# One dense tile of short pieces instead of two, with the tests' classification and the fetched rows' copies moved

## The chip, the cores and the metric

The kernel runs on one core of a Trainium2 chip. The metric is the device time of one execution in microseconds; three executions are quoted by their median. One further execution was profiled, and every row below is from that one.

## What is computed

Attention over 4 sequences of 768 tokens and 8 heads of 64 (a causal window of 128 keys, and 4 sink keys that every query sees), then a soft mixture of experts, then a mixture in which each token goes to one expert:

```python
x = attention(q, k, v)                      # 3072 x 512
logits = x @ phi                            # 8 experts x 4 slots
slot_in = softmax(logits, axis=0).T @ x     # 32 x 512
slot_out[e] = relu(slot_in[e] @ w1[e]) @ w2[e]
x = softmax(logits, axis=1) @ slot_out      # 3072 x 512

idx = argmax(normed(x) @ normed(expert_emb).T / tau)
p = softmax of those logits at idx
out = p * (relu(x @ w1[idx]) @ w2[idx])     # float32
```

After the soft mixture every row of x is a combination of the same 32 slot rows, and with the reference's inputs all 3072 tokens choose the same expert in the second mixture.

## The kernel before

The first 200 us are the attention and the soft mixture; the change touches them in one place, `tokens()`, which puts the combining weights of the tokens into the order of the output tiles. The rest is the second mixture for the one chosen expert, and its method sets the words used below.

The combining weights stand in `cstack` (96 rows that carry a high and a low part, 32 rows that are filled late), a column for each of the 3072 tokens, in 24 tiles of 128. The expert's first layer, pulled through the slots, stands in `gst`. So a product of a 128-column piece of `gst` with 512 columns of `cstack` gives the hidden layer before its relu for 128 units and 512 tokens. That is a **test** (`hidden()`, T, L1192): 8 unit groups f by 6 token groups g, 48 in all. The kernel doesn't keep the hidden layer. It counts signs: `sign(n)` (c0 to c47) goes over the test on ScalarE (Sign with an accumulated sum, L1201) or VectorE (L1203), by the list `ON_ACT`. A unit that is positive for every token counted is linear, and needs no relu; one that is positive for none is left out; the others are **mixed**.

Early tokens see few keys, and their hidden layer has many sign changes. The first `ND` = 2 tiles are therefore **dense**: tile 0 and tile 1 hold the first 64 tokens of each of the four sequences, and their signs are not counted. Their relu is kept by `relu_d()` (h, L1209, ScalarE) and its rounding rest by `rest_d()` (i, L1216, VectorE), in two parts of `hd`; `products()` (D, L1228) multiplies them with the expert's whole second layer, 24 products for a tile. Tiles 2 and 3 hold the second 64 tokens of each sequence, tiles 4 to 23 are 128 rows in a row each. `rows_of(t)` tells which rows of the output a tile stands for: two pieces of 64 rows for tiles 0 to 3, else one of 128.

**Classification** is made in two parts, `ca` for the first `NA` = 5 unit groups and `cb` for the other three: a reduction of the counts and comparisons on VectorE (L1249 to L1253), a product on POOL, two on TensorE that number the mixed units, and `pos` on VectorE (L1262). `select(f)` (e0 to e7) turns a group's numbers into a matrix of 0 and 1; `gather()` (L1279) multiplies those with `gt`, so that up to 256 columns hold the mixed units' first layer, copied to `gc` by ScalarE (L1281). `SEL_ACT` = (7,) puts the last select onto ScalarE, as two operations. `rows()` (L1288) brings the numbers into a column, `fetch()` makes indices of them (`ii`, L1304, VectorE) and issues two indirect DMAs on POOL (L1307), which read the mixed units' rows of the second layer into `w2g`: first 128, and in the second half at most 10 more. `split_rows()` copies and splits them (w2c, ScalarE L1311 and VectorE L1313; `wx`, ScalarE L1315, and part of `gws`, VectorE L1317). `linear()` (lin) sums the linear units on TensorE (8 products, L1326), copies on ScalarE (L1328, L1334) and finishes `gws` on VectorE (L1336).

Output tiles 2 to 23 are made by `outputs(t)` (y2 to y23): four products into one PSUM bank (L1382), three with `w2c` and the mixed units' hidden layer of this token group (`hm`, made by `mixed(g)`: TensorE L1348, ScalarE L1350, VectorE L1352), and a fourth with `gws` and `cstack`, whose last 32 rows `extra(g)` writes (TensorE L1361, ScalarE `hx` L1364, VectorE L1366). The last tile is made in two halves of 256 columns (L1378). `stores()` (st) takes the tiles in order: ScalarE evicts with the gate as its scale into one of six buffers `ot` (L1234), and SyncE issues one DMA for each piece of `rows_of(t)` (L1236).

Every engine works in order. PSUM is eight banks handed out first in, first out by `take()` and `give()`. The order is written by hand: each name in the string `ORDER` advances that generator to its next `yield`, so a step that stands early in the string stands early on its engine. At the end, when the count of mixed units is over `CAP` = 138, or when tokens have other experts, a branch ("rest") does the remaining work.

## Time and profile before

| | us |
|---|---|
| three executions | 277.50, 277.81, 278.89; median 277.81 |
| the profiled execution | 277.48 |
| its span | 275.7 |
| TensorE busy in the span | 260.6 (95%) |
| ScalarE, VectorE, POOL busy | 193.6, 184.4, 168.7 |
| the tests | 211 to 234 |
| first product with gws | 249.19 |
| last product | 268.54 |

The whole span's shares are a mean over stages with different limits: attention, the soft mixture, the tests, the chain from the last classification to `gws`, and the output. What a step is worth has to be read in its stage, by what waits and for whom. The durations of a row are of the one profiled execution.

### The profile page before, as it was taken

To read this page: it belongs to the slowest core of one execution; us is meant where nothing else is said; L and a number is where in the kernel's file an instruction comes from. 1 tells how busy PE (TensorE), PEld (TensorE's weight loads), DVE (VectorE), ACT (ScalarE), POOL (GpSimd) and SP (SyncE) were. 2 spreads that over 40 slices of the span, in tenths; PEclk is the share of its full clock that TensorE was granted. 3 is DMA by queue.
4 is the path that set the end of the run, shared out by engine and by line. 5 is a ranking of instruction groups with operands and counts; after the bars stand their busy time and mean duration, and the time that the engine had idled before them with its cause. 6 is when DMAs were issued, how large, how long until landed. Compare 5 with 4: busy or idle time off the path is not lost. (4 is left out here: it accounts for less than half of the span.)

```text
span 275.7 us, 8854 instructions
## 1 busy us (share of the span) xinstructions
PE 260.6 (95%) x3257; PEld 165.7 (60%) x3257; DVE 184.4 (67%) x556; ACT 193.6 (70%) x679; POOL 168.7 (61%) x394
## 2 busy tenths in 40 slices
PE   7987989999999999999999999999999999999990
PEld 5645646665666665666655563333477774777880
DVE  6786768888888898887985144526326889673410
ACT  2676988889898898989988522311227998677981
POOL 4398999999999999999999440001203995110000
PEclk9999999999999999999999999999999999999997
DMA  7894598756797467889924498999059000036884
GB/s 242 307 421 172 182 349 295 253 153 217 295 410 253 146 194 231 313 283 370 411 81 152 134 424 316 420 440 393 13 185 407 19 1 1 2 94 146 306 293 160
DMA packets 15198, 65.37 MB, mean 237 GB/s; under 512 B 2736, under 2 KB 3248, under 8 KB 11568
## 3 DMA queue, kind: packets, MB, share of 16 engines
q1 hardware_dynamic: 13600, 63.77, 62.7%
q10 hardware_dynamic: 1392, 0.48, 0.7%
q8 instruction: 27, 0.44, 0.6%
q0 software_dynamic: 160, 0.52, 0.6%
q14 instruction: 19, 0.16, 0.2%
HBM read 58.48 MB, written 6.29 MB: 235 GB/s over the span
## 5 line engine op out<-in xcount | busy, mean ns | idle before, releaser
L255 ACT ACTIVATE pr<-sc,nm 128x132 f32<-128x132 f32 x192 | 68.6, 373 | 5.8 <-DVE rs L260 3.8
L265 POOL TENSOR_TENSOR pr<-pr,rs 128x528 f32<-128x528 f32 x48 | 51.2, 1067 | 10.4 <-DVE rs L261 9.7
L233 DVE COPY_PREDICATED sc<-t_le_q,sc 128x512 f32<-128x512 uint32 x48 | 33.3, 695 | 10.1 <-PE sc L218 8.0
L255 ACT ACTIVATION_READ_ACCUMULATOR pr<-sc,nm 128x1 f32 x192 | 40.0, 209 | 0.0
L218 PE MATMUL sc<-qk 64*32 64x164 f32 (+4 forms) x1536 | 36.2, 294 | 2.1 <-DMA qk<-in_qkv_dram 1.9
L241 DVE TENSOR_REDUCE sc<-sc 128x4 f32<-128x528 f32 x48 | 33.9, 706 | 1.1
L289 ACT ACTIVATE raw<-m 128x512 f32<-128x512 f32 x48 | 28.6, 603 | 6.1 <-PE m L284 2.8
L295 POOL TENSOR_SCALAR_AFFINE_SELECT pt<-raw 128x512 f32<-128x512 f32 x48 | 30.6, 639 | 0.4
L339 PE MATMUL xa<-pt,v 128*64 128x256 f32 (+1 forms) x256 | 29.5, 361 | 0.7 <-POOL pt L299 0.7
L218 PEld LDWEIGHTS sc<-qk 64*32 64x32 f32 x1536 | 21.4, 106 | 14.4 <-issue 7.0
L284 PE MATMUL m<-ident,pr 128*128 128x128 f32 x192 | 28.9, 276 | 0.6 <-POOL pr L265 0.6
L284 PEld LDWEIGHTS m<-ident,pr 128*128 128x128 f32 x192 | 22.0, 141 | 4.1 <-POOL pr L265 2.1
L339 PEld LDWEIGHTS xa<-pt,v 128*64 128x64 f32 x256 | 15.6, 136 | 10.8 <-issue 3.3
L810 POOL CAST scr<-scr 128x256 fp32r<-128x256 f32 x6 | 2.4, 402 | 30.7 <-DVE scr L806 30.0
L373 ACT ACTIVATE xtok<-m 128x512 f32<-128x512 f32 (+1 forms) x32 | 15.8, 497 | 6.6 <-PE m L356 6.1
L302 POOL TENSOR_SCALAR_AFFINE_SELECT pt<-raw 128x256 f32<-128x256 f32 x48 | 19.5, 408 | 0.7
L339 PE MATMUL xb<-pt,v 128*64 128x128 f32 (+1 forms) x192 | 18.1, 315 | 0.0
L1169 POOL TENSOR_TENSOR w2h<-w2t,ones 128x512 fp32r<-128x512 f32 x8 | 8.3, 1042 | 15.3 <-PE b L1019 15.3
L356 PE MATMUL m<-ident,xt 128*128 128x128 f32 x96 | 15.8, 275 | 0.0
L1201 ACT ACTIVATE junk<-b 128x512 f32<-128x512 f32 (+1 forms) x26 | 14.8, 568 | 0.5
L1382 PE MATMUL b<-w2c,hm 128*128 128x512 f32 x45 | 14.7, 399 | 0.0
L339 PEld LDWEIGHTS xb<-pt,v 128*64 128x64 f32 x192 | 10.7, 136 | 5.0 <-issue 3.8
(327 smaller groups left out, 566.5 us busy)
## 6 DMA issues: line engine op xcount, KB each, us to landing
w<-in_m1w_dram SPq DMA_DIRECT2D x19, 1024.0 KB, 8.1
qk<-in_qkv_dram SPq DMA_DIRECT2D x15, 780.0 KB, 5.7
w<-in_m1w_dram SPq DMA_DIRECT2D x4, 2048.0 KB, 12.8
v<-in_qkv_dram SPq DMA_DIRECT2D x16, 448.0 KB, 3.5
out_dram<-ot SPq DMA_DIRECT2D x19, 256.0 KB, 2.6
x<-in_m1w_dram SPq DMA_DIRECT2D x4, 1024.0 KB, 8.1
w1t<-in_m2w_dram SPq DMA_DIRECT2D x4, 512.0 KB, 5.2
w2t<-in_m2w_dram SPq DMA_DIRECT2D x4, 512.0 KB, 8.9
```

Source lines behind the costliest of these rows:

```text
L218: pe.matmul(sc[r0:r0 + 32, h, o + lo:o + hi], lhsT=lhsT, rhs=qk[hp:hp + 64, k0 + lo:k0 + hi], start=True, stop=True)
L233: dve.copy_predicated(mv[:, :, :, 0:128], mk.to_broadcast([128, 2, 2, 128]), bv[:, :, :, 124:252])
L241: dve.tensor_reduce(mx, mv[:, :, :, 0:UW], axis=X, op=ALU.max, negate=True)
L255: act.activation(out=pr[:, h, i2, :], in_=mv[:, h, i2, 0:UW], func=AF.Exp, bias=nm[:, h, i2:i2 + 1], scale=0.125, accum_out=sm[:, h, i2, 0:1])
L265: pool.tensor_tensor(out=pr, in0=pr, in1=sm.rearrange("p h (i o) -> p h i o", o=1).to_broadcast([128, 2, 2, UW]), op=ALU.mult)
L284: pe.transpose(ps[:, h, i2, :], pr[:, h, i2, 0:128], ident)
L289: act.activation(out=raw, in_=tp_t.pop(u), func=AF.Copy)
L295: pool.affine_select(out=pt[:, :, :, 0, :], in_=raw_t[u], pattern=[[0, 2], [0, 2], [1, 128]], compare_op=ALU.is_ge, fill=0.0, base=0, chan ...
L302: pool.affine_select(out=pt_t[u][:, :, 0, 1, :], in_=raw_t[u][:, :, 1, :], pattern=[[0, 2], [-1, 128]], compare_op=ALU.is_gt, fill=0.0, ba ...
L339: pe.matmul(o[64 * h:64 * h + 64, c0:c0 + 128 * (l1 - l0)], lhsT=v[:, j, h, :], rhs=mv[:, h, 128 * l0:128 * l1], start=False, stop=last, s ...
L356: pe.transpose(ps[:, 128 * t:128 * t + 128], xt[:, 128 * (t0 + t):128 * (t0 + t) + 128], ident)
L373: act.activation(out=dst, in_=src, func=AF.Copy)
```

## The change

The dense tiles go from two to one. `rows_of` now lays tiles 0 to 3 out in four pieces of 32 rows: tile t holds tokens 32t to 32t+31 of each of the four sequences, so the dense tile 0 has the first 32 tokens of each, and tiles 1 to 3, now ordinary output tiles, the next 96. `tokens()` follows that layout. The relu and rest of the dense part go from 256 columns to 128, the first group's signs from 256 to 384, the dense products from 48 to 24 and the output tiles' products from 88 to 92. The output DMAs go from 29 to 36: 16 pieces of 32 rows and 20 tiles, where 8 pieces of 64 rows, 19 tiles and two halves stood; the last tile is made and stored whole. `NA` goes from 5 to 6, so that the first classification waits for six groups' signs and the second has two; the last select goes from ScalarE to VectorE. `ORDER` is written anew from the middle on. Lines 1192 to 1236 move by one or two and the outputs' line from L1382 to L1376.

```diff
-ND = 2
+ND = 1
+NF = 4

     def rows_of(t):
-        if t < 2 * ND:
-            h, b2 = divmod(t, ND)
-            return [(slice(64 * k, 64 * k + 64), S * (2 * b2 + k) + 64 * h, 64) for k in range(2)]
-        b, i = divmod(t - 2 * ND, NB - 1)
+        if t < NF:
+            return [(slice(32 * b, 32 * b + 32), S * b + 32 * t, 32) for b in range(B)]
+        b, i = divmod(t - NF, NB - 1)
         return [(slice(0, 128), S * b + 128 * (i + 1), 128)]

         def tokens(b2):
...
             for b in range(2):
-                for k in range(2):
-                    pe.matmul(tp[64 * b:64 * b + 64, 32 * k:32 * k + 32], lhsT=lt_all[:, 2 * b2 + b, 64 * k:64 * k + 64], ...)
+                r = 64 * b2 + 32 * b
+                for k in range(NF):
+                    pe.matmul(tp[r:r + 32, 32 * k:32 * k + 32], lhsT=lt_all[:, 2 * b2 + b, 32 * k:32 * k + 32], ...)
...
-            act.activation(out=c_tok[:, b2:b2 + ND + 1:ND, :], in_=tp[:, 0:64]..., func=AF.Copy)
+            act.activation(out=c_tok[rs, 0:NF, :], in_=tp[rs, 0:32 * NF]..., func=AF.Copy)
...
     def products():
-        for t in range(ND):
-            tok = slice(128 * t, 128 * t + 128)
-            y = hold(("y", t), 1)
-            for f in range(8):
-                for k, w in ((0, w2h), (0, w2l), (1, w2h)):
-                    pe.matmul(y, lhsT=hd[:, k, f, tok], rhs=w[:, f], ...)
+        ys = [hold(("y", t), 1) for t in range(ND)]
+        for f in range(8):
+            for k, w in ((0, w2h), (0, w2l), (1, w2h)):
+                for t in range(ND):
+                    pe.matmul(ys[t], lhsT=hd[:, k, f, 128 * t:128 * t + 128], rhs=w[:, f], ...)

-    def store(t, c):
+    def store(t):
-        act.activation(out=ot[:, c], in_=y[:, c], func=AF.Copy, scale=gsel[:, t:t + 1])
+        act.activation(out=ot, in_=y, func=AF.Copy, scale=gsel[:, t:t + 1])
         for ps, r, n in rows_of(t):
-            sp.dma_start(out=out[r:r + n, c], in_=ot[ps, c])
+            sp.dma_start(out=out[r:r + n, :], in_=ot[ps])

     def outputs(t):
-        if t == NTILE - 1:
-            for c in (slice(0, 256), slice(256, 512)):
...
-    SEL_ACT = (7,)
-    NA = 5
+    SEL_ACT = ()
+    NA = 6
     ORDER = """
...
-        c32 c33 c34 ca c35 h u0 ca w2 T T T D D c37 c38 ca ca i c36 c39 T D T T c40 T D T c41 c44 h e1 e0 T T c43 e2 D gat gat T gat e3 gat lin c45 c46 i c42
+        c35 ca h u0 ca w2 T T D T ca ca e0 e1 e2 c37 c38 i c36 c39 T D T T D c40 T T D c41 c44 h T T c43 gat gat T gat e3 gat lin c45 c46 c42 c47 cb e4 e5 D
...
```

The first place is TensorE around the end of the gather (L1279) and the rows (L1288); L1326 and L1332 are the linear part, L1361 and L1348 `extra` and `mixed`, `m` or a `b` with a number is a PSUM bank. Before:

```order
L1228 MATMUL m<-w2h,hd 128x512
L1279 MATMUL b_3980<-sel,gt 128x256 x3
L1326 MATMUL b_3988<-w2t,gta 32x512 x4
L1228 MATMUL m<-w2h,hd 128x512
L1228 MATMUL m<-w2l,hd 128x512
L1288 MATMUL b_4039<-ident,gc 128x1 x2
L1361 MATMUL b_4047<-cstack,gc 128x512
L1348 MATMUL b_4050<-cstack,gc 128x512
L1361 MATMUL b_4052<-cstack,gc 128x512
```

After, on the same engine:

```order
L1229 MATMUL b_3849<-w2l,hd 128x512
L1279 MATMUL b_3975<-sel,gt 128x256 x2
L1229 MATMUL b_3849<-w2h,hd 128x512 x2
L1288 MATMUL m<-ident,gc 128x1 x2
L1326 MATMUL b_3983<-w2t,gta 32x512 x4
L1348 MATMUL b_4040<-cstack,gc 128x512
L1361 MATMUL b_4042<-cstack,gc 128x512
L1229 MATMUL b_3849<-w2l,hd 128x512
L1332 MATMUL b_4045<-gwb,rep_153 128x512
```

The rows stand behind the gather and two dense products now, and the second half of the linear part, which stood ahead of them, behind; a single first `mixed` and `extra` go ahead of the linear part's last product.

The second place is ScalarE from the first fetched rows on (L1311, then L1315 `wx`), with L1334 a copy to `gws`, L1364 `hx`, L1350 `hm` and L1234 (after: L1235) the evictions of output tiles. Before:

```order
L1311 ACTIVATE w2c<-w2g 128x512
L1334 ACTIVATE gws<-b_4084 96x512
L1364 ACTIVATE hx<-b_4088,xm 32x512
L1234 ACTIVATE ot<-m,gsel 128x512
L1315 ACTIVATE wx_3633<-w2g,xm 32x512
L1234 ACTIVATE ot<-m,gsel 128x512
L1234 ACTIVATE ot<-b_4098,gsel 128x512
L1350 ACTIVATE hm<-b_4143 128x512
```

After, on the same engine:

```order
L1311 ACTIVATE w2c<-w2g 128x512
L1315 ACTIVATE wx_3641<-w2g,xm 32x512
L1334 ACTIVATE gws<-b_4045 96x512
L1364 ACTIVATE hx<-m,xm 32x512
L1350 ACTIVATE hm<-b_4087 128x512
L1235 ACTIVATE ot<-b_3849,gsel 128x512
L1235 ACTIVATE ot<-m,gsel 128x512
L1235 ACTIVATE ot<-b_4077,gsel 128x512
L1235 ACTIVATE ot<-b_4080,gsel 128x512
L1364 ACTIVATE hx<-b_4115,xm 32x512
```

`wx` stands directly behind the first fetched rows' copy, where `gws`, an `hx` and an eviction stood between; the dense tile's eviction, the first one, is behind all five.

The third place is SyncE's queue from the last weights to the branch at the end (`aint` is the branch's word). Before:

```order
L993 DMA w2t<-in_m2w_dram 128x1024
L1236 DMA out_dram<-ot 64x512 x8
L1236 DMA out_dram<-ot 128x512 x19
L1236 DMA out_dram<-ot 128x256 x2
L1577 TENSOR_LOAD aint
L1577 ISA x2
```

After, on the same engine:

```order
L995 DMA w2t<-in_m2w_dram 128x1024
L1237 DMA out_dram<-ot 32x512 x16
L1237 DMA out_dram<-ot 128x512 x20
L1571 TENSOR_LOAD aint
L1571 ISA x2
```

Eight pieces of 64 rows have become sixteen of 32, and the halves of the last tile are gone.

## Rows read from the trace of the kernel before

**Rows 1.** The page's first line.

```profile
span 275.7 us, 8854 instructions
```

**Rows 2.** Busy time by stretches: from:to, length, then each engine with its instructions.

```profile
core 0: us, PE busy (x) PEld busy (x) DVE busy (x) ACT busy (x) POOL busy (x), PEclk, DMA share, GB/s
163.00:190.00 27.00, 26.91 (x250) 10.19 (x248) 12.32 (x31) 5.99 (x13) 0.80 (x2) 1.00 0.97 397
222.20:233.80 11.60, 10.97 (x51) 7.34 (x51) 10.64 (x35) 11.19 (x36) 8.91 (x10) 1.00 0.00 1
249.20:268.90 19.70, 19.61 (x89) 15.95 (x89) 5.98 (x22) 16.67 (x27) 0.00 (x0) 1.00 0.78 256
```

**Rows 3.** Timeline, 236 to 250 us: start, duration, engine, line, operation, [idle before, releaser].

```profile
236.70 0.51 ACT L1270 ACTIVATE sel<-sq,ones 128x256 fp32r<-128x256 f32 x1
...
237.26 0.19 PEld L1279 LDWEIGHTS b<-sel,gt 128*128 128x128 f32 x1 [0.24 <-ACT sel L1270]
...
237.58 1.06 PE L1326 MATMUL b<-w2t,gta 128*32 128x512 f32 x8
...
239.68 0.34 DVE L1304 TENSOR_SCALAR ii<-b,ebase 128x1 int32<-128x1 f32 x2 [1.36 <-PE b L1288]
...
240.19 1.18 POOL L1307 DMA_INDIRECT w2g<-in_m2w_dram,ii  x1 [4.74 <-DVE cnt L1295]
...
241.68 0.95 POOL L1307 DMA_INDIRECT w2g<-in_m2w_dram,ii  x1 [0.30 <-issue]
...
243.72 0.63 ACT L1311 ACTIVATE w2c<-w2g 128x512 fp32r<-128x512 f32 x1 [0.61 <-DMA w2g<-in_m2w_dram,ii]
...
246.28 0.72 ACT L1315 ACTIVATE wx<-w2g,xm 32x512 fp32r<-32x512 f32 x1
...
248.44 0.69 DVE L1336 TENSOR_TENSOR gws<-b,gws 32x512 fp32r<-32x512 f32 x1
...
249.19 0.50 PE L1382 MATMUL b<-gws,cstack 128*128 128x512 f32 x1
...
249.73 0.69 ACT L1234 ACTIVATE ot<-b,gsel 128x512 f32<-128x512 f32 x1 [0.63 <-PE b L1382]
```

**Rows 4.** Timeline, 256 to 269 us, ScalarE and TensorE.

```profile
256.97 0.68 ACT L1364 ACTIVATE hx<-b,xm 32x512 fp32r<-32x512 f32 x1
...
268.54 0.27 PE L1378 MATMUL b<-gws,cstack 128*128 128x256 f32 x1
```

**Rows 5.** Tile `ot`, 263.4 to 270 us: ns min/median/max, first and last start; the landing.

```profile
L1236 SPq DMA_DIRECT2D out_dram<-ot x9: 332/383/1888, 263.6 to 269.8; - x9
...
DMA to landing us min/median/max: 2.9/3.9/4.3
```

**Rows 6.** Busy time by stretches of 1 us, columns as in rows 2.

```profile
251.00:252.00 1.00, 1.00 (x6) 0.82 (x5) 0.25 (x1) 0.88 (x2) 0.00 (x0) 1.00 0.97 203
258.00:259.00 1.00, 1.00 (x6) 0.82 (x5) 0.97 (x2) 0.97 (x3) 0.00 (x0) 1.00 0.97 363
265.00:266.00 1.00, 1.00 (x6) 0.82 (x5) 0.23 (x2) 0.87 (x2) 0.00 (x0) 1.00 0.11 33
```

**Rows 7.** Tile `ot`, 255.1 to 263.3 us, whole tiles of 128 rows.

```profile
L1236 SPq DMA_DIRECT2D out_dram<-ot x10: 332/332/333, 255.2 to 263.0; - x10
...
DMA to landing us min/median/max: 2.0/2.2/4.3
```

**Rows 8.** Tile `ot`, 249 to 253.4 us, pieces of 64 rows.

```profile
L1236 SPq DMA_DIRECT2D out_dram<-ot x6: 466/526/590, 249.1 to 252.8; - x6
...
DMA to landing us min/median/max: 2.2/2.3/2.4
```

**Rows 9.** Groups by line and form on ScalarE, 211.2 to 234.3 us: busy, mean ns.

```profile
L1201 ACT ACTIVATE junk<-b 128x512 f32<-128x512 f32 x22 | 13.2, 601 | 0.4
...
L1209 ACT ACTIVATE hd<-b 128x256 fp32r<-128x256 f32 x7 | 2.6, 378 | 0.0
L1201 ACT ACTIVATE junk<-b 128x256 f32<-128x256 f32 x4 | 1.5, 384 | 0.0
```

**Rows 10.** Tile `w2g`: the two indirect DMAs' landing.

```profile
DMA to landing us min/median/max: 3.5/3.6/3.8
```

More of the change, by code (lines that the diff above doesn't have):

```diff
@@ L751, in tokens @@
             tp = take()
+            rs = slice(64 * b2, 64 * b2 + 64)
+            for b in range(2):
+                r = 64 * b2 + 32 * b
+                for k in range(NF):
+                    pe.matmul(tp[r:r + 32, 32 * k:32 * k + 32], lhsT=lt_all[:, 2 * b2 + b, 32 * k:32 * k + 32], rhs=ident[0:96, 0:32], start=True, stop=True)
             for b in range(2):
                 for k in range(2):
-                    pe.matmul(tp[64 * b:64 * b + 64, 32 * k:32 * k + 32], lhsT=lt_all[:, 2 * b2 + b, 64 * k:64 * k + 64], rhs=ident[0:96, 0:32], start=True, stop=True)
-            for b in range(2):
-                for k in range(2):
-                    o = 64 + 192 * b + 96 * k
+                    o = 128 + 192 * b + 96 * k
                     pe.transpose(tp[:, o:o + 96], lt_all[:, 2 * b2 + b, 128 * k:128 * k + 128], ident[0:96, 0:96])
             yield
-            act.activation(out=c_tok[:, b2:b2 + ND + 1:ND, :], in_=tp[:, 0:64].rearrange("p (k s) -> p k s", k=2), func=AF.Copy)
+            act.activation(out=c_tok[rs, 0:NF, :], in_=tp[rs, 0:32 * NF].rearrange("p (k s) -> p k s", k=NF), func=AF.Copy)
             for b in range(2):
-                o = 64 + 192 * b
-                c0 = 2 * ND + 5 * (2 * b2 + b)
+                o = 128 + 192 * b
+                c0 = NF + 5 * (2 * b2 + b)
                 act.activation(out=c_tok[:, c0 + 1:c0 + 4:2, :], in_=tp[:, o + 32:o + 96].rearrange("p (g s) -> p g s", g=2), func=AF.Copy)
@@ L1222, in products @@
         hd, w2h, w2l = room("hd"), room("w2h"), room("w2l")
[L1223 to L1228 removed]
+        ys = [hold(("y", t), 1) for t in range(ND)]
+        for f in range(8):
+            for k, w in ((0, w2h), (0, w2l), (1, w2h)):
+                for t in range(ND):
+                    pe.matmul(ys[t], lhsT=hd[:, k, f, 128 * t:128 * t + 128], rhs=w[:, f], start=(f == 0 and k == 0 and w is w2h), stop=(f == 7 and k == 1))
                     yield
[L1231 removed]
+    def store(t):
         y = held["y", t]
         ot = Q.sb.tile([128, DM], F32, tag="ot", bufs=6, name="ot")
[L1234 removed]
+        act.activation(out=ot, in_=y, func=AF.Copy, scale=gsel[:, t:t + 1])
         for ps, r, n in rows_of(t):
[L1236 removed]
+            sp.dma_start(out=out[r:r + n, :], in_=ot[ps])
         drop(("y", t))
@@ L1240, in stores @@
         for t in range(NTILE):
-            for c in (slice(0, DM),) if t < NTILE - 1 else (slice(0, 256), slice(256, 512)):
-                store(t, c)
-                yield
+            store(t)
+            yield
     def classify(fs):
@@ L1372, in outputs @@
         tok = slice(128 * r, 128 * r + 128)
-        y = hold(("y", t), 1 if t < NTILE - 1 else 2)
+        y = hold(("y", t), 1)
         hm = hm_t[g]
-        if t == NTILE - 1:
-            for c in (slice(0, 256), slice(256, 512)):
-                for k, (a, b) in enumerate(((hm[:, 0, tok], Q.w2c[:, 0, c]), (hm[:, 1, tok], Q.w2c[:, 0, c]), (hm[:, 0, tok], Q.w2c[:, 1, c]), (cs_t[0][:, 128 * t:128 * t + 128], Q.gws[:, c]))):
-                    pe.matmul(y[:, c], lhsT=a, rhs=b, start=(k == 0), stop=(k == 3))
-                yield
-            return
         for k, (a, b) in enumerate(((hm[:, 0, tok], Q.w2c[:, 0]), (hm[:, 1, tok], Q.w2c[:, 0]), (hm[:, 0, tok], Q.w2c[:, 1]), (cs_t[0][:, 128 * t:128 * t + 128], Q.gws))):
@@ L1417, in kernel_body @@
-        c47 e4 cb cb D D D gat cb cb e7 e5 D D num D e6 gate gate gate gat gat gat lin D D gat gate row fetch fetch fetch fetch fetch x1 m1 x0 lin num gate x1
-        x1 x0 m1 m0 x0 m2 m2 m2 m0 m0 w2c D D D D D D lin lin D x2 D D D D x2 x2 w2c y2 y5 D D D y2 D y3 y5 y3 D D D y7 y2 D st w2c m1 w2c y3 y6 y4 lin y2 y5
-        y5 y6 st st m3 y4 y4 y3 y9 m3 m3 y7 y7 y10 y4 y6 y6 st st st x3 y8 y9 y8 x3 flag x3 y8 y8 y7 st st y15 x4 y10 y9 y9 y15 y12 y12 y13 m4 y13 st st x4
-        flag x4 m4 m4 y10 y10 y11 y13 y11 y11 y11 st st y16 y12 x5 y12 y15 y18 y13 y16 y14 y14 y14 y14 x5 st st st y16 y16 y15 m5 st flag x5 y18 y18 st m5 y17
@@ new lines, in kernel_body @@
+        cb D cb gat gat cb e6 e7 D num D gat gat i gate gate gat D D row fetch fetch fetch fetch fetch lin gate num gate lin m0 x0 D lin D m0 m0 x0 gate x0 m1
+        D D m1 m1 w2c D x1 w2c w2c lin lin w2c x1 x1 y1 y1 y2 y2 y3 y3 y4 y4 m2 y1 y2 m2 y3 y4 st m2 y1 st y2 st x2 y3 st x2 x2 y4 st y5 y5 y5 y5 st y6 y6 y6
+        y6 st y7 y7 y7 y7 st y8 y8 y8 y8 st y9 y9 m3 y9 y9 m3 m3 st y10 y10 x3 y10 y10 x3 x3 st flag y11 y11 y11 y11 st y12 y12 y12 y12 st y13 y13 m4 y13 y13
+        m4 m4 st flag y14 y14 x4 y14 y14 x4 x4 st y15 y15 y15 y15 st y16 y16 y16 y16 st flag y17 y17 m5 y17 y17 m5 m5 st y18 y18 x5 y18 y18 x5 x5 st flag y19
@@ L1422, in kernel_body @@
+        y19 y19 y19 st y20 y20 y20 y20 st flag hint y21 y21 y21 y21 st y22 y22 y22 y22 st y23 y23 y23 y23 st
         """.split()
```

10 lines of the change are left out of this document (4 added, 6 removed).

## Prediction, made before the changed kernel was run

> **What bounds the kernel now.** The profiled execution took 277.48 us, 0.33 below the median of the three runs (277.81); its span is 275.7 us [rows 1], so 1.78 lie outside the span. I sum against 277.48 and add the difference to the median at the end. About 0.5% (1.39 us) is what a measurement of this kernel can tell from no change.
>
> I read the busy time by stretches first. TensorE is busy 26.91 of 27.0 us while the soft mixture runs, 10.97 of 11.6 us in the tests, and 19.61 of 19.7 us in the output stretch [rows 2]. Its granted clock is 1.00, the higher of the two levels (2.4 GHz), in all three. In the tests stretch ScalarE (11.19 us) and VectorE (10.64 us) are as full as TensorE, so the eviction of the tests sets its pace. The reader should then see what starts the output stretch: a chain of small steps, pos, select, gather, gc, rows, ii, indirect fetch, w2c and gws, of which the last, VectorE's L1336, releases TensorE at 249.19 after 0.55 us of idling [rows 3]. From there TensorE streams to its last product at 268.54 [rows 4]; ScalarE evicts, SyncE issues the last store at 269.8 and the span ends 5.9 us later [rows 1, 5].
>
> One more engine hides in that stretch. The DMA engines are 0.78 busy on average [rows 2], and their speed depends on the piece. In 251 to 252 us, with 64-row pieces in flight, they are 0.97 busy for 203 GB/s; in 258 to 259, with whole tiles, 0.97 busy for 363 GB/s [rows 6]. A 64-row piece (131 kB) thus occupies them for 131/203 = 0.646 us, a 128-row tile (262 kB) for 0.72: half the rows cost nearly the whole time. SyncE's issue of one piece shows the same slope: 0.332 us for a whole tile [rows 7], 0.526 median and 0.590 at most for a 64-row piece [rows 8]. Before, eight such pieces pass without holding anybody up. After, there are sixteen of 32 rows.
>
> **The change part by part.**
>
> *The tests.* Relu of the dense part goes from 256 to 128 columns. From 601 ns at 512 columns and 384 at 256 [rows 9], a column costs 0.85 ns, 128 of them 0.108 us. Eight relus save 0.87 us on ScalarE, the four first-group signs there grow by 0.43, and VectorE's rest shrinks alike; 24 dense products of some 0.23 us leave TensorE, which has cover here. Against it, the first classification now sums six units' tests, two tests further, and its pos and three selects stand straight behind it on VectorE, ahead of tests c37 and c38, whose banks TensorE and ScalarE wait for. I take -0.2 us for the start of the second classification, with bounds of -0.8 (relu saving, half of it as VectorE's) and +0.3 (VectorE's idling for pos).
>
> *The last select.* Before, it is two ScalarE operations, the second 0.51 us from 236.70, and the gather's last weight load waits 0.24 us for it [rows 3]. On VectorE it is one operation behind the other selects, and TensorE works on dense products till then. I take -0.3: the wait and a hand-over.
>
> *The rows.* Before, their small products stand behind eight products of the linear part (1.06 us from 237.58) and dense products; VectorE's ii starts at 239.68 after 1.36 us of waiting for them [rows 3]. After, they stand behind the gather and two dense products (which cover the copy gc), and the second four linear products behind them. That gives -0.9 (those 1.06 less a hand-over); with the two terms above, -1.4, and the first indirect DMA at 240.19 - 1.4 = 238.8. The linear part loses 0.3 by it, but its result is wanted only at gws, later than the fetched rows.
>
> *Fetched rows ahead of other copies.* The first half of w2g is used 3.53 us after its issue (243.72 against 240.19), the second issue comes 1.49 after the first [rows 3], and the longer landing of the two is 3.8 [rows 10]: 238.8 + 1.5 + 3.8 = 244.1. Before, the copy wx waited until 246.28 behind an eviction and hx. After, wx follows at once (0.72), then the copy to gws (0.60), then VectorE's two subtractions of 0.69: 244.1 + 0.72 + 0.60 + 1.38 = 246.8, where 249.13 stood. So gws is ready 2.3 us earlier; 1.5 to 3 in bounds.
>
> *The tile more.* From the first gws product on, before has 82 products' worth in 268.54 - 249.19 + 0.12 = 19.5 us, 0.237 each [rows 3, 4]; after it has 86.5: 20.5 us. If nothing else waits, the stream ends at 246.85 + 20.5 = 267.35, 1.3 us earlier. The last tile is no longer in halves; its eviction starts 0.54 after its last product starts and takes 0.69 [rows 3]: 267.1 + 1.23 = 268.35. The last store then needs a landing. The last nine stores before took 3.9 us (median), behind one issue of 1.888 us [rows 5], during which the DMA engines stood nearly idle (0.11 in 265 to 266 [rows 6]); without that, 2.2 to 2.4 are usual [rows 7, 8]. With 2.4, then 2.0 from landing to the span's end (5.9 less 3.9) and 1.78: 274.5. That is the bound by TensorE alone.
>
> *The sixteen pieces.* ScalarE's queue after the second fetch is wx, gws, hx, hm and the dense tile's eviction; five at 0.60 back to back (the mean of 128x512 in rows 9) end at 247.15, when the first piece can be issued. Sixteen pieces at c each, the last landing 2.2 after its turn [rows 8], give 247.15 + 15c + 2.2 = 249.35 + 15c for the end of the four split tiles. There are six output buffers: tile 9 needs the buffer of tile 3. Behind tile 9's eviction on ScalarE stands hx of the fourth group (0.68 alone [rows 4], 0.60 back to back), behind that VectorE's 0.69 for cstack (the duration of L1336 [rows 3]), and behind that, on TensorE, the last product of tile 13 and all that follows. From that product's start to the last one's start are 42.5 products, 10.07 us. So the run is 249.35 + 15c, plus 2.0 (eviction, hx, cstack, hand-overs), plus 10.07 + 1.23 + 4.4 + 1.78, or 268.8 + 15c. It comes level with before at c = 0.58, is 0.5% faster below 0.485, 0.5% slower above 0.67, and TensorE's own bound takes over below 0.38.
>
> No row shows a 32-row piece. The bounds of c: below, a whole tile's issue, 0.332 [rows 7], and a gap that I estimate at 0.05, together 0.38; above, the step from 0.332 to 0.526 made once more, 0.72, with the gap 0.77. Between stand 0.57 (the 64-row issue [rows 8] with the gap) and 0.646 (the DMA engines' time for a 64-row piece, if a quarter of the rows again halves the speed). I take 0.62, next to the later of these two, since the queue is empty at the first pieces.
>
> The row above says that a half-height piece keeps the engines nearly as long as a whole tile. The Trainium skill has the same direction as a rule, in "DMA: Bandwidth & Descriptors", section "Rules for kernel authors": two transfers to disjoint halves of the partitions serialize, and one of 128 partitions should be used. It speaks against this change; it gives no price for a quarter.
>
> *At nothing.* tokens() makes 16 small products of 32 rows where 8 stood, and more evictions, while the weights' DMA is 0.97 busy [rows 2]; TensorE's other work there covers it too, and with both gone eight more small products cost some tenths. Waits of POOL and SyncE's queue elsewhere are not moved.
>
> **Sum.** 268.8 + 15 x 0.62 = 278.1, or 0.6 above 277.48; on the median's scale 278.4. Its own range, for c of 0.57 to 0.68 and the tests' bounds, is 276.9 to 279.5.
>
> **The rivals.**
>
> *Pieces overlap.* Four pieces of a tile touch four disjoint quarters, so they might run side by side, and an issue might cost what a whole tile's does. Then TensorE is the bound: 274.5, on the median's scale 274.8. For it: 0.332 is what nearly all whole tiles take [rows 7]. Against it: the 64-row pieces of one tile didn't overlap, 203 GB/s at 0.97 [rows 6]. The Trainium skill's linear law ("DMA: Bandwidth & Descriptors", section "Anatomy of one DMA", fitted for POOL's queue: some 2 us and bytes by 436 GB/s) would give 64 KB only 0.15 us of transfer, an estimate from that page, and so this case; the 203 GB/s of rows 6 already break it for pieces of 128 KB.
>
> *Pieces cost more still.* Fewer rows each time made the issue longer. At 0.77, SyncE's queue holds the buffers until 260.9, ScalarE stands before tile 9, hx and cstack come later by it, and the run is 280.4, or 280.7 by the median: slower. It decides from c = 0.67. For it: the slope from 128 to 64 rows, and one issue of 1.888 with nothing else to blame [rows 5]. Against it: the smallest 64-row issue took 0.466 [rows 8].
>
> *The earlier gws doesn't come.* If the fetched rows gain only 1 us, the pieces start a microsecond later, and the forecast becomes 279.4; it lies in the slower part of the forecast's chance.
>
> *Not what it says.* Fewer dense tokens give more mixed units: the reference's inputs have 103 with 64 tokens taken out and 124 with 32, of room for 138. Above 138 a branch of tens of microseconds would run. 0.02.
>
> **How the numbers follow.** Forecast 0.50 (of it 0.34 within 0.5%, 0.12 slower, 0.04 faster), overlap 0.28 (0.25 faster, 0.03 within), dearer 0.20 (slower), branch 0.02 (slower). Faster 0.29, same 0.37, slower 0.34. The range runs from 274.6, which takes in most of the overlap case, to 281.0, which takes in the dearer one's 280.7; the forecast's own, 277.2 to 279.8 by the median, stands beside it.
>
> **What would show it.** L1279's last load no longer waits for ScalarE; the first L1307 near 238.8; wx near 244; gws near 246.8. The 16 issues on SyncE run without gaps from 247 to 256 or 257, the DMA engines near 0.97 at little over 100 GB/s. ScalarE waits for a DMA ahead of tile 9 (and shorter ahead of 6 to 8) until 258 or 259, and TensorE then waits at tile 13. If no eviction waits for a DMA, c was below 0.4 and the forecast is wrong by over 3 us; if SyncE's issues last over 0.7, the dearer case holds.

## The result

The changed kernel is slower by 1.1%. Twenty executions of each gave medians of 282.34 us (changed) and 279.49 us (before); the ratio, which leaves out the most disturbed executions, is 1.0114, with a 95% interval of 1.0078 to 1.0149. On the 277.81 us of before that is 3.2 us, between 2.2 and 4.1. The prediction was 278.4, "within 0.5%" the likeliest, and a range that ended at 281.0.

In ten of the sixteen profiles of this document TensorE's granted clock falls to 0.50 (1.2 GHz, the lower of its levels) for a few microseconds early in the attention, which no line of the change touches. The engine has waited for inputs before it (below it is busy 0.47 of the 2.00 us in which the clock falls), but the wait alone doesn't decide it: e3_tests, below, waited longer there and kept the clock. The profile of the changed kernel is of such an execution, and that of before is not. It shows in stretches of 2 us (from:to, length, busy time and instructions of PE, PEld, DVE, ACT and POOL, the granted clock, the DMA share and GB/s). Before, then changed:

```profile
24.00:26.00 2.00, 2.00 (x41) 1.44 (x49) 1.85 (x7) 1.37 (x3) 1.14 (x2) 1.00 0.06 25
```

```profile
22.00:24.00 2.00, 0.47 (x25) 0.50 (x31) 0.00 (x0) 0.86 (x6) 1.75 (x7) 0.89 0.85 347
24.00:26.00 2.00, 2.00 (x26) 1.22 (x9) 1.03 (x3) 0.00 (x0) 0.00 (x0) 0.50 0.11 44
```

So of the 4.56 us between the two profiled executions (282.04 and 277.48), 2.53 are there before the first test's product starts (213.22 against 210.69). All the stages below are therefore counted from that product. From it to the start of the last eviction the changed kernel takes 60.60 us and before 58.58: 2.0 us more, and that is what the change does in this trace. The ends are alike (6.4 us from that start to the end of the span). 2.0 lies below the interval of the measured 2.2 to 4.1; what else is in the median I come back to with the runs.

### The profile page after: what moved, and what is told of

It is laid out like the page before. It is cut to its first block, busy times and chain, and to the rows that moved or that the text cites. A ratio compares the mean times of both kernels' runs of the same rounds, so it can differ in the third digit from the quotient of the medians.

```text
span 280.2 us, 8846 instructions
## 1 busy us (share of the span) xinstructions
PE 259.1 (92%) x3249; PEld 162.8 (58%) x3249; DVE 184.9 (66%) x557; ACT 192.6 (69%) x676; POOL 168.7 (60%) x394
## 5 line engine op out<-in xcount | busy, mean ns | idle before, releaser
L219 PE MATMUL sc<-qk 64*32 64x164 f32 (+4 forms) x1536 | 36.8, 298 | 3.0 <-DMA qk<-in_qkv_dram 2.7
L1376 PE MATMUL b<-w2c,hm 128*128 128x512 f32 x54 | 16.5, 398 | 0.0
L1203 ACT ACTIVATE junk<-b 128x512 f32<-128x512 f32 (+1 forms) x23 | 13.4, 583 | 2.8 <-PE b L1194 2.5
L1235 ACT ACTIVATE ot<-b,gsel 128x512 f32<-128x512 f32 x19 | 12.8, 689 | 2.3 <-PE b L1376 1.2
```

The source lines that it names most:

```text
L219: pe.matmul(sc[r0:r0 + 32, h, o + lo:o + hi], lhsT=lhsT, rhs=qk[hp:hp + 64, k0 + lo:k0 + hi], start=True, stop=True)
L1376: pe.matmul(y, lhsT=a, rhs=b, start=(k == 0), stop=(k == 3))
```

## The profile after

TensorE's busy time by stage shows where the time goes. These are three stretches of before that answer to [rows 2] (tests, first part; end of the tests to w2c; to gws), and then five of the changed kernel, each some 2.5 us later:

```profile
211.20:222.20 11.00, 11.00 (x57) 8.15 (x57) 9.95 (x29) 10.34 (x36) 10.61 (x10) 1.00 0.26 105
233.80:244.40 10.60, 10.55 (x57) 6.92 (x49) 7.76 (x29) 7.16 (x14) 2.48 (x3) 1.00 0.13 44
244.40:249.20 4.80, 4.68 (x21) 3.50 (x20) 3.46 (x5) 3.21 (x5) 0.00 (x0) 1.00 0.29 69
```

```profile
213.70:224.70 11.00, 10.47 (x53) 7.03 (x51) 10.23 (x30) 10.40 (x38) 10.61 (x10) 1.00 0.27 110
224.70:236.30 11.60, 8.42 (x36) 5.84 (x35) 8.51 (x30) 8.82 (x29) 9.00 (x10) 1.00 0.00 0
236.30:246.90 10.60, 10.22 (x54) 5.80 (x53) 7.85 (x33) 6.22 (x16) 2.42 (x3) 1.00 0.12 36
246.90:251.50 4.60, 3.47 (x14) 2.40 (x14) 3.41 (x6) 3.42 (x6) 0.00 (x0) 1.00 0.10 37
251.50:273.30 21.80, 20.62 (x88) 16.24 (x89) 8.32 (x25) 18.29 (x30) 0.00 (x0) 1.00 0.76 253
```

With the tests' second part and the output stretch of [rows 2], TensorE before idles 0.00 + 0.63 + 0.05 + 0.12 + 0.09 = 0.9 us in all of these 58: it is the bound, and the dense products fill what the chain of small steps leaves. After, it idles 0.53 + 3.18 + 0.38 + 1.13 + 1.18 = 6.4 us. The change took 24 products away and put 4.5 in, some 4.6 us at the 0.237 us of a product in the stream. Its busy time fell by 3.6 us only (56.8 to 53.2; a product behind a wait, for one thing, shows up to 0.50 us, below at 235.38 and 251.50). The idle time grew by 5.5. The difference, 1.9, is the loss.

The largest loss is in the tests, 3.18 us in one stretch. The timeline of the changed kernel there (start, duration, engine, line, operation, [idle before, releaser]):

```profile
230.62 0.24 DVE L1249 TENSOR_REDUCE ac<-acc 128x12 f32<-128x84 f32 x1 [1.13 <-ACT junk L1203]
...
231.64 0.36 PE L1259 MATMUL b<-mix,tri 128*128 128x6 f32 x2 [1.68 <-DVE mix L1252]
...
232.65 2.07 DVE L1272 TENSOR_SCALAR sel<-ki,pos 128x256 fp32r<-128x256 f32 x3
...
233.03 1.28 POOL L1172 TENSOR_TENSOR w2l<-w2t,w2h 128x512 fp32r<-128x512 f32 x1
...
234.64 0.68 DVE L1205 TENSOR_SCALAR_CACHE_REDUCE junk<-b 128x512 f32<-128x512 f32 x1
...
235.38 0.50 PE L1194 MATMUL b<-cstack,gst 128*128 128x512 f32 x1 [1.48 <-DVE junk L1205]
...
235.98 0.60 ACT L1203 ACTIVATE junk<-b 128x512 f32<-128x512 f32 x1 [1.73 <-PE b L1194]
```

The second of the three selects by itself:

```profile
233.02 1.44 DVE L1272 TENSOR_SCALAR sel<-ki,pos 128x256 fp32r<-128x256 f32 x1
```

VectorE first stands 1.13 us for ScalarE's sign of the sixth group; TensorE has the numbering products of that classification next in its queue, so it stands too, 1.68 us, with tests behind them. Then the three selects take 2.07 us together (two take 0.60 and 0.62 later, at 239.39 and 240.15). One of them has 1.44 of it: it starts with POOL's subtraction and ends 0.15 us behind that one's end. Only then comes test c37, whose bank TensorE needs (1.48 us), and ScalarE idles 1.73 us for the next test. The second classification starts 25.27 us after the first test; before it was 23.75.

The chain to gws afterwards:

```profile
242.98 1.18 POOL L1307 DMA_INDIRECT w2g<-in_m2w_dram,ii  x1 [3.54 <-DVE n L961]
...
248.59 0.72 ACT L1315 ACTIVATE wx<-w2g,xm 32x512 fp32r<-32x512 f32 x1 [1.09 <-DMA w2g<-in_m2w_dram,ii]
...
250.67 0.69 DVE L1317 TENSOR_TENSOR gws<-w2g,wx 32x512 fp32r<-32x512 f32 x1
...
251.50 0.47 PE L1376 MATMUL m<-gws,cstack 128*128 128x512 f32 x1 [0.65 <-DVE gws L1317]
```

From the second classification to the first indirect DMA it takes 4.49 us (5.75 before, up to the 240.19 of [rows 3]), from there until gws is written 8.38 (8.94 before). These steps are as meant; they give back the 1.5 us that the tests lost, and 0.3 more: gws is written 38.14 us after the first test, before 38.44.

The stores of tiles 0 to 3, from the view of tile `ot` between 251.9 and 259.4 us (ns min/median/max, first and last start), answer to [rows 8], and two stretches of 1 us to [rows 6]:

```profile
L1237 SPq DMA_DIRECT2D out_dram<-ot x16: 366/422/437, 252.0 to 259.0; - x16
...
DMA to landing us min/median/max: 1.7/1.7/1.8
```

```profile
255.00:256.00 1.00, 1.00 (x6) 0.79 (x5) 0.30 (x1) 1.00 (x3) 0.00 (x0) 1.00 0.56 137
262.00:263.00 1.00, 0.00 (x0) 0.00 (x0) 0.70 (x1) 0.97 (x3) 0.00 (x0) 1.00 1.04 391
```

A 32-row piece issues in 0.422 us, less than a 64-row one, and follows the last at 7.0 / 15 = 0.466 us. The DMA engines are 0.56 busy with them: SyncE sets the pace, they don't. What follows is the wait that the prediction described:

```profile
257.06 0.69 ACT L1235 ACTIVATE ot<-b,gsel 128x512 f32<-128x512 f32 x1 [0.62 <-DMA out_dram<-ot]
...
258.92 0.69 ACT L1235 ACTIVATE ot<-m,gsel 128x512 f32<-128x512 f32 x1 [1.17 <-DMA out_dram<-ot]
...
260.86 0.69 ACT L1235 ACTIVATE ot<-b,gsel 128x512 f32<-128x512 f32 x1 [0.76 <-PE b L1376]
...
261.57 0.68 ACT L1364 ACTIVATE hx<-b,xm 32x512 fp32r<-32x512 f32 x1
...
262.28 0.70 DVE L1366 SCALAR_TENSOR_TENSOR cstack<-b,hx 32x512 fp32r<-32x512 f32 x1 [1.46 <-ACT hx L1364]
...
263.03 0.49 PE L1376 MATMUL b<-gws,cstack 128*128 128x512 f32 x1 [1.18 <-DVE cstack L1366]
```

ScalarE waits for buffers three times, before tiles 7, 8 and 9, 2.55 us in all. The view puts the third wait down to a product, but tile 9's own products were done by 257.8; it ends with the landing of tile 3's last piece, which was issued at 258.98 and landed 1.8 us later. hx stands behind tile 9's eviction, and TensorE waits 1.18 us at tile 13's last product, in the empty stretch 262 to 263.

## The experiments

Two theories came out of this. **A**: the order in the tests (a classification of six groups, selects in one block) costs some 1.5 us. **B**: the sixteen pieces cost another 1.2 to 1.7 us through the buffers. The rival to both is my prediction's picture, in which the chain alone counts and dense products are under cover. All times in this table are from the start of the first test's product in that kernel's trace; the ratio is of timed runs to the kernel before on the same chip.

| kernel | second classification | first gws product | last eviction starts | ratio (95%) |
|---|---|---|---|---|
| before | 23.75 | 38.50 | 58.58 | |
| changed | 25.27 | 38.28 | 60.60 | 1.0114 (1.0078 to 1.0149) |
| changed, again (e0) | 25.21 | 38.33 | 60.61 | 1.0111 (1.0077 to 1.0145) |
| e5_selects | 24.67 | 37.42 | 59.72 | 1.0074 (1.0023 to 1.0124) |
| e3_tests | 23.73 | 37.03 | 59.33 | 1.0075 (1.0025 to 1.0124) |
| e14_whole | 25.46 | 38.23 | 58.94 | 1.0094 (1.0041 to 1.0148) |
| e16_both | 23.75 | 38.22 | 58.93 | 0.9942 (0.9897 to 0.9987) |
| e15_ten | 24.04 | 37.48 | 58.25 | 0.9967 (0.9916 to 1.0018) |
| e9_chain | 23.76 | 38.15 | 58.14 | 1.0073 (1.0030 to 1.0116) |
| e10_double | 26.22 | 39.88 | 62.17 | (medians 284.57 and 277.51) |
| e8_hx | 23.95 | 38.04 | 60.01 | 1.0045 (1.0001 to 1.0089) |
| e13_flag | 24.06 | 37.57 | 59.32 | 1.0042 (0.9991 to 1.0093) |
| e4_before32 | 23.72 | 38.59 | 58.67 | 1.0055 (1.0004 to 1.0105) |
| e11_null | 23.94 | 38.72 | 58.81 | 0.9989 (0.9923 to 1.0054) |

The early fall of the clock lies ahead of the first test and so outside these marks. In five of these profiles the clock fell to 0.50 for 3.4 us between the first test and the first gws product too: in e0, e5_selects and e14_whole in the last tests, in e16_both and e8_hx in the chain behind them.

**The changed kernel again.**

> The changed kernel again, as the base of this chip's comparisons: 1.008 to 1.015 of the kernel before. In the trace, without any dip of TensorE's clock, the first test stands 0.4 us earlier than before, VectorE's second classification some 1.5 us later, gws within 0.3 us of before, and the last product 2 us later than before.

It repeats: the same three marks within 0.06 us, the same ratio. That its clock fell in the tests moved none of the marks:

```profile
231.60:234.80 3.20, 2.90 (x7) 1.79 (x7) 3.17 (x8) 1.37 (x4) 1.75 (x2) 0.50 0.00 0
```

In that stretch VectorE is the fuller engine (3.17 of 3.20 us).

**The tests' order (A).** The first classification goes back to five groups, its selects between the later tests:

```diff
-    NA = 6
+    NA = 5
...
-        c35 ca h u0 ca w2 T T D T ca ca e0 e1 e2 c37 c38 i c36 ... T T c43 gat gat T gat e3 gat lin c45 c46 c42 c47 cb e4 e5 D
+        ca c35 h u0 ca w2 T T D T c37 c38 ca ca i c36 ... e1 e0 T T c43 e2 gat gat T gat e3 gat lin c45 c46 c42 c47 e4 cb D
...
```

> The changed kernel with the first classification over five groups again, its selects spread between the later tests as before. Theory that VectorE's order in the tests made it slower: TensorE's and ScalarE's waits of 1.5 to 1.7 us near the 37th test are gone, gws is 1.5 to 2 us earlier and the run 1.5 to 2 us faster than the changed kernel, level with before or 0.5 us off. Theory that the pieces bind: gws is earlier, but the run gains under 0.5 us because the stores take it back.

The second classification is back at 23.73, before's 23.75, gws comes 1.25 us earlier than in the changed kernel, and the last eviction starts 1.27 us earlier, a little under the 1.5 to 2 expected (the timed ratio is lower by 0.0036, which is within the intervals). Nothing is taken back on the way, and nothing of the pieces' wait goes: TensorE's waits from 248 to 271 us (waiter, what for, total, times, longest):

```profile
PE b L1376 <- DVE cstack L1366: 1.2, 1, 1.2
PE m L1376 <- DVE gws L1317: 0.4, 1, 0.4
```

**Which half of the order.** Six groups as changed, but pos and the selects spread:

```diff
-        ... T T D T ca ca e0 e1 e2 c37 c38 i c36 ... c44 h T T c43 gat
+        ... T T D T c37 c38 ca ca i c36 ... c44 h e1 e0 T T c43 e2 gat
```

> The changed kernel, the first classification over six groups as changed, but its pos and selects spread between the later tests. If the block of three selects on VectorE made the loss: nearly all of e3_tests' gain, 1.0 to 1.5 us against the changed kernel. If the later classification itself (it waits for ScalarE's sign of the 35th test): under 0.5 us, and TensorE still waits 1.7 us for its numbering products.

The second classification starts at 24.67, 0.6 us earlier than in the changed kernel, and the last eviction 0.88 earlier, of the 1.27 that e3_tests gains. That lies between the two expectations. TensorE still waits 1.5 us for its numbering products, as the second one has it. How the loss divides between the block and the later classification is not shown: behind that wait the clock fell in this profile while TensorE was busy throughout, and a part of the 0.9 us that remain may come of it.

```profile
232.80:236.10 3.30, 3.30 (x9) 2.63 (x9) 2.80 (x9) 1.38 (x4) 1.90 (x2) 0.50 0.01 2
```

Nor does a run part the block from POOL's subtraction beside it, which was not moved.

**The pieces (B).** The changed kernel, but tiles 0 to 3 stored as whole tiles:

```diff
-        for ps, r, n in rows_of(t):
+        for ps, r, n in rows_of(t) if t >= NF else [(slice(0, 128), S * t, 128)]:
```

> The changed kernel with tiles 0 to 3 each stored as one whole tile of 128 consecutive rows, so that these rows of the output stand in another order; everything else as changed. It takes the sixteen pieces away. Theory that they cost the output stretch through the buffers: TensorE's 1.2 us at tile 13 are gone, no eviction waits for a DMA, and the run is 1.2 to 1.5 us faster than the changed kernel, 1.003 to 1.006 of before. Theory that the rest is at fault: under 0.4 us.

From the first gws product to the last eviction it is 20.7 us where the changed kernel has 22.3: 1.6 us, a little over the 1.2 that TensorE waited. Its waits from 251 to 273 us are one row:

```profile
PE m L1376 <- DVE gws L1317: 0.4, 1, 0.4
```

The timed ratio, 1.0094, is only 0.002 lower than the changed kernel's; its interval holds both theories' values, so the trace carries this point.

**Both undone.**

> e3_tests with tiles 0 to 3 each stored as one whole tile of 128 consecutive rows (these rows stand in another order in the output). It is the limit of what the pieces can give back. If the causes add: first gws product to the last one's start 20.2 us as in e14_whole, first test to last eviction 57.7 us, 0.9 us less than before, 0.996 to 0.999. If a new wait comes up: 58.3 or more.

```diff
-    NA = 6
+    NA = 5
...
-        for ps, r, n in rows_of(t):
+        for ps, r, n in rows_of(t) if t >= NF else [(slice(0, 128), S * t, 128)]:
```

(with e3_tests' order). 0.9942: faster than before, clear of 1. Its profile doesn't show it, with a last eviction at 58.93 (before 58.58): there TensorE's clock fell in the chain, and the first gws product came at 38.22, where e3_tests, without that fall, has 37.03:

```profile
237.00:240.00 3.00, 3.00 (x14) 2.10 (x17) 1.13 (x7) 1.67 (x2) 0.02 (x1) 0.51 0.00 0
```

From the first gws product to the last eviction it took 20.71 us, as in e14_whole. So in the trace the two losses stand in different stretches and each goes with its own edit. By an estimate from these two, e3_tests' 37.03 and this 20.71 make 57.7 us, as expected, 0.8 less than before: the smaller dense part would pay without the two new waits. No trace shows that sum in one execution, and the timed ratio may not be all the change's own: the executions of e16_both were granted 0.996 of the clock (median), those of before on that chip 0.992, which is 1.1 us of a span of 275.

**The layout that keeps the rows in place.** Tokens 32 to 127 of the sequences stand one after another in tiles 1 to 3, which makes two pieces each of 32, 64 or 96 rows; tile 0 keeps four:

```diff
+            at = [divmod(128 * (t - 1) + 32 * j, 96) for j in range(4)]
+            for b in range(B):
+                js = [j for j in range(4) if at[j][0] == b]
+                if js:
+                    out_.append((slice(32 * js[0], 32 * js[-1] + 32), S * b + 32 + at[js[0]][1], 32 * len(js)))
```

> The kernel with the tests' order as before (e3_tests), and tokens 32 to 127 laid out in tiles 1 to 3 one sequence after another, so that these tiles are two pieces each of 32, 64 or 96 rows: ten pieces in all for tiles 0 to 3 where the changed kernel has sixteen. If the two causes (VectorE's order in the tests, the pieces) add: tile 13's wait is gone, first test to last eviction 57.7 to 58.2 us (changed kernel 60.6, before 58.6), 0.997 to 1.001 of before. If the pieces still hold the buffers: 59 or more, 1.004.

Tile 13's wait is gone (the longest on TensorE is 0.5, for gws), evictions wait 1.1 us for buffers where it was 2.55, and the last eviction starts at 58.25, 0.3 before the kernel before and 0.05 past the bound expected. 0.9967, interval 0.9916 to 1.0018: the best version with the whole output in place, by the median of the ratio faster than both, by its interval not told apart from before.

**The chain's edits alone, in the kernel before.** This run tests the prediction's picture:

```diff
-    SEL_ACT = (7,)
+    SEL_ACT = ()
...
-        ... gat gat gat lin D D gat gate row fetch fetch fetch fetch fetch x1 m1 x0 lin num ... m0 w2c D D D D D D lin lin D x2
+        ... gat gat gat D D gat gate row fetch fetch fetch fetch fetch lin x1 m1 x0 lin num ... m0 w2c w2c w2c D D D D D D lin lin D lin w2c x2
```

> The kernel before with the chain's edits alone: the last select on VectorE, the rows ahead of the second half of the linear part, the copy wx and both of VectorE's subtractions straight behind the fetched rows. Both dense tiles stay. Theory of the prediction (the chain of small steps sets the start of the output stretch): gws 1.5 to 2 us earlier, the run 1.2 to 1.5 faster, 0.995. Rival, from the busy time of TensorE in the kernel before (idle for 0.9 us in all from 211 us to its last product): TensorE has the dense products to do anyway, so its stream can shorten by its idle time alone; the run gains 0.3 to 0.6 us, 0.998 to 0.999.

gws is written 1.7 us earlier than before, within the prediction's bounds of 1.5 to 3. But TensorE doesn't come for it:

```profile
249.74 0.69 DVE L1317 TENSOR_TENSOR gws<-w2g,wx 32x512 fp32r<-32x512 f32 x1
...
251.86 0.39 PE L1382 MATMUL b<-gws,cstack 128*128 128x512 f32 x1
```

It works through dense products, and has no idle time at all in the two stretches around it:

```profile
240.00:251.80 11.80, 11.80 (x55) 8.37 (x55) 9.03 (x23) 9.20 (x15) 2.13 (x2) 1.00 0.16 48
251.80:271.00 19.20, 19.20 (x89) 15.68 (x88) 6.07 (x23) 16.71 (x28) 0.00 (x0) 1.00 0.84 268
```

The last eviction starts 0.44 us earlier, as the rival said, though not by idle time alone: 0.63 of the 0.9 us lie in the tests, which this edit leaves as they are. The timed ratio goes the other way (1.0073); the trace from the first test on doesn't explain that. Its profile has the early fall of the clock and starts the tests 3.0 us later than before's (213.71 against 210.69); whether its executions have it more often stays open.

**Dense products put back.** Each of the 24 is made twice:

```diff
-                    pe.matmul(ys[t], lhsT=hd[:, k, f, ...], rhs=w[:, f], start=(...), stop=(...))
+                    for z in range(2):
+                        pe.matmul(ys[t], lhsT=hd[:, k, f, ...], rhs=w[:, f], start=(... and z == 0), stop=(... and z == 1))
```

> The changed kernel with each of the 24 dense products made twice into the same bank, so the dense tile's rows come out doubled; it puts back the TensorE time that the second dense tile had. If these products lie under the chain of small steps: within 0.6 us of the changed kernel, 1.009 to 1.014 of before. If TensorE's time counts there: 24 x 0.237 = 5.7 us more, 1.031.

The last eviction moved by 1.6 us, neither 0.6 nor 5.7. So of 5.7 us of products, as many as the change removed, 1.6 count in its own schedule, 0.95 of that already in the tests; the rest goes into idle time.

**hx ahead of tile 9's eviction, and the flag step later.** Two tries to move the wait at tile 13 away by order alone, on e3_tests:

```diff
-        ... st y5 y5 y5 y5 st y6 y6 y6 y6 st ... y9 y9 m3 y9 y9 m3 m3 st y10 y10 x3 y10 y10 x3 x3 st
+        ... st y5 y5 m3 y5 y5 m3 m3 st y6 y6 x3 y6 y6 x3 x3 st ... y9 y9 y9 y9 st y10 y10 y10 y10 st
```

> The kernel with the tests' order as before (e3_tests), and the fourth group's mixed and extra steps made four tiles earlier, so that hx no longer stands on ScalarE behind tile 9's eviction, which waits for tile 3's four stores. Theory that the sixteen pieces cost the output stretch through this wait: TensorE's wait of about 1.2 us at tile 13 is gone and the run is 0.8 to 1.2 us faster than e3_tests, 1.003 to 1.005 of before. Rival: the stores themselves are late, the wait moves to the banks, and under 0.3 us is gained.

```diff
-        ... st flag y17 y17 m5 y17 y17 m5 m5 st y18
+        ... st y17 y17 m5 y17 y17 m5 m5 st flag y18
```

> e8_hx, with the flag step whose small product on TensorE waited 1.0 us for VectorE moved two tiles later. If that wait was what took the place of tile 13's: TensorE streams from the first gws product to the last without a wait over 0.5 us, 0.8 to 1.0 us faster than e8_hx and level with before, 0.999 to 1.003. If evictions or buffers hold it: another wait on TensorE of the same size, and no gain.

From the first gws product to the last eviction they take 21.97 and 21.75 us, e3_tests 22.30. In e8_hx a small product of the flag step waited 1.0 us in its place; in e13_flag a wait of 0.7 for cstack came up. Order alone gives back a third of the pieces' 1.6 us at most: the rival of each was nearer. (That e8_hx has its first gws product a microsecond later than e3_tests goes with the fall of the clock in its chain.)

**Small pieces in the kernel before.**

```diff
+            for o in range(0, n, 32 if n < 128 else 128):
+                m = min(n, 32) if n < 128 else n
+                sp.dma_start(out=out[r + o:r + o + m, c], in_=ot[ps.start + o:ps.start + o + m, c])
```

> The kernel before, but the eight stores of 64 rows are sixteen of 32, and nothing else. Theory that a 32-row piece is cheap (0.47 us from issue to issue, the DMA engines about 0.57 busy, as in the trace of the changed kernel): the sixteen take 7.5 us of SyncE instead of 4.6, mostly between evictions that are spread over 7 us anyhow, and the run is within 0.5 us of before. Theory of the prediction (0.62 and more): tile 8's and 9's evictions wait for buffers and 1 us or more is lost.

```profile
L1238 SPq DMA_DIRECT2D out_dram<-ot x16: 314/422/437, 245.8 to 253.7; - x16
```

The same 0.422 us: the price belongs to the piece, not to its surroundings. The last eviction stands 0.09 us from before, since no eviction before tile 20 waited for a buffer; the timed ratio (1.0055, from 1.0004) is at the edge of no difference.

**One DMA for a tile's four stretches.** Meant to take the pieces away:

```diff
+            sp.dma_start(out=out.rearrange("(b s) d -> b s d", b=B)[:, 32 * t:32 * t + 32, :], in_=ot)
```

> The changed kernel, but tiles 0 to 3 are each stored by one DMA of 128 rows (the destination is four stretches of 32 rows) instead of four. Theory that the pieces on SyncE matter: no eviction waits for a DMA ahead of tile 9, the wait of 1.18 us at tile 13 is gone, and the run is 1.2 us faster than the changed kernel, 1.003 to 1.007 of before. Theory that the tests alone made it slower: within 0.4 us of the changed kernel. The chain to gws is as in the changed kernel by both.

> Both edits: one DMA for each of tiles 0 to 3, and the tests' order as before. If the two causes add: 2.7 to 3.2 us faster than the changed kernel, 0.5 to 1.2 us faster than before (0.996 to 0.998). If the pieces only bind where gws is early, this gains more over the tests' edit alone than the one DMA gains over the changed kernel: 1.8 against 1.2 us.

Neither theory was tested: 1.0424 (1.0365 to 1.0484) and, with the tests' order, 1.0345 (1.0284 to 1.0406). The four DMAs take so long that evictions wait 8.7 us for buffers. Tile `ot` of e1_one_dma, and the first whole tile behind the four:

```profile
L1237 SPq DMA_DIRECT2D out_dram<-ot x4: 544/755/867, 251.3 to 253.6; - x4
...
  DMA out_dram<-ot: 8.7, 4
```

```profile
L1240 SPq DMA_DIRECT2D out_dram<-ot x1: 2702/2702/2702, 254.6 to 254.6; - x1
...
DMA to landing us min/median/max: 12.3/12.3/12.3
```

The trace has no landing of the four themselves. With all of them in flight the DMA engines are 0.24 busy, about four of the sixteen:

```profile
255.00:256.00 1.00, 1.00 (x6) 0.77 (x6) 0.00 (x0) 0.13 (x1) 0.00 (x0) 1.00 0.24 90
```

**A program that does the same.** One memset of 0.06 us twice, in the kernel before.

> The kernel before with one memset of a single column made twice, 0.06 us on VectorE and nothing else. It measures how far two programs that do the same work differ by the falls of TensorE's clock between 22 and 29 us, which the trace shows in some executions. If these falls don't depend on the program: 0.998 to 1.002. If they do: 1.003 or more, with the medians further apart than the lowest times.

0.9989, and an interval of 1.3% in width. So half a per cent is about the least that such comparisons tell apart. The two signs that were named disagree: the ratio says no difference, but the medians of all executions are 1.69 us apart (280.61 and 278.92) and the lowest times 0.05. So a harmless edit may move the median, and no run tells whether it did. The two profiles differ by 0.23 us at the last eviction, and a difference of that size in the table, e15_ten's 0.33 nearly, says little.

The 1.2 us between the trace's 2.0 and the median's 3.2 are open. The clock is large enough for them. On e0's chip the executions of the changed kernel were granted 0.987 of it (median), those of before 0.995, and 0.008 of a span of 279 us is 2.2 us. The fall in the tests is not the place, as e0 shows. The early fall may be: the ten profiles that have it start the first test at 212.4 to 214.9 us, the six without it at 209.7 to 211.2. Nine of the twelve profiles with the new layout have it and one of four with the old, a profile each. Whether the change brings it on is not shown.

## Why the prediction was wrong

**The tests.** This is the step that failed and made the kernel slower: the start of the second classification was put at -0.2 us with an upper bound of +0.3, and measured +1.5. Undoing it alone (e3_tests) gave 1.27 us back at the last eviction. The mechanism stood in the prediction (pos and three selects ahead of c37 and c38); the price was guessed and not worked out. Of the waits that made the price it had only an idling of VectorE, at 0.3 us. The runs showed VectorE's 1.13 us for ScalarE's sign of the sixth group, TensorE's 1.68 behind it, and a select that took 1.44 beside POOL's subtraction. The trace of before shows the last of these in small, two selects beside such a subtraction and two without one:

```profile
230.12 1.30 POOL L1170 TENSOR_TENSOR w2l<-w2t,w2h 128x512 fp32r<-128x512 f32 x1
...
230.81 1.02 DVE L1272 TENSOR_SCALAR sel<-ki,pos 128x256 fp32r<-128x256 f32 x2
...
232.36 0.61 DVE L1272 TENSOR_SCALAR sel<-ki,pos 128x256 fp32r<-128x256 f32 x2
```

So gws, forecast 2.3 us earlier, was written 0.3 earlier.

**The picture of the bound.** The prediction read each wait of the chain as the start of the output stretch, and took [rows 3]'s 0.55 us of idling before gws as its sign. It had TensorE's stages in [rows 2], but didn't add up the idle time over the whole stretch, 0.9 us. That sum says that a shorter chain alone gives before little (e9_chain: 0.44), and that the change makes the chain the bound by taking work away. The prediction has TensorE's "cover" for the tests, the last select and tokens(); that the dense products were the cover of the whole chain was missed. In the changed kernel the chain does set the start (TensorE idles 0.38 and 1.13 us ahead of gws), so this alone did not spoil the sum.

**The last select, the rows, the fetched rows.** Second classification to first indirect DMA: forecast -1.2, measured -1.26, right. From there to gws: forecast -0.9, measured -0.56, short by a third; the fetch landed later (4.1 at most, not 3.8).

**The tile more.** 86.5 products for 82: from the first gws product to the last eviction, without the pieces (e14_whole), 20.7 us against 20.1 before; by the prediction's terms 20.8. Right.

**The pieces.** The mechanism was right to the tile: six buffers, tile 9, hx, cstack, tile 13. The size was off in the other direction, 0.62 us forecast, 0.466 measured, 2.3 us over fifteen. With the measured size the prediction's own sum is 275.8 us, faster than before. The trend from 128 to 64 rows, in issue time and in DMA speed, did not go on: 32-row pieces move at 137 / 0.56 = 245 GB/s of busy time, above the 209 of [rows 6].

**The end.** I took a landing of 2.4 us for the last store, without the 3.9 of [rows 5], 1.5 us gained. The span ended 5.7 us after the last issue (274.5), not 4.4: the store landed after 2.9 us, and 2.8 more followed where 2.0 were taken.

So, from the forecast's 278.1 to the profiled 282.04, on top of the 2.5 us upstream: first piece +2.3 (1.7 of it from the tests), pieces -2.3, their landing -0.4, the stretch behind +0.5, the end +1.3. That the forecast lay as near as it did is luck: two misses of 2.3 us cancelled, and the forecast's 0.6 came out at 2.0 in the trace. "Dearer pieces", the rival with the right sign, was not the cause.

## What to carry to other kernels

Add up the idle time of the engine that looks busiest over the whole stretch before costing a step of a chain beside it: that sum is about what a shorter chain can give, and removing work from that engine gives only what the chain leaves. When work moves between queues, write out what then stands in front of each buffer's release: here the later classification with its block of selects cost 1.3 us and the pieces 1.6, and either is more than the 0.8 us that the smaller dense part gives without them, by the estimate above. A saving that vanishes may still be there: undo the new waits one by one and together, as e16_both did, before giving the idea up. And look where the clock fell in each profile before dividing a difference of half a microsecond between two causes.

## What the runs showed of the hardware

Stores of a tile by SyncE took 0.332 us to issue at 128 rows, 0.526 at 64 and 0.422 at 32 (medians), and the DMA engines moved them at some 374, 209 and 245 GB/s of busy time: halves are worse than quarters here.

Four DMAs, each to four stretches of 32 rows, kept the DMA engines 0.24 busy at 90 GB/s, and the whole tile issued behind them landed after 12.3 us; the sixteen separate pieces landed after 1.7 each. The Trainium skill has a rule for this in "DMA: Bandwidth & Descriptors", section "Rules for kernel authors": an outermost dimension of fewer than 16 confines a DMA to at most that many engines. The share of 0.24, about 4 of 16, agrees with it.

A VectorE select, 0.34 us by itself, ended 0.15 us behind POOL's subtraction of two tensors wherever it ran beside one: it took 1.44 us so in the changed kernel (POOL from 233.03 for 1.28), 1.21 in e5_selects, 0.94 in e3_tests and 0.75 in before.
